# Second feed-forward block in token pieces of 512 and 384, with the output weights stationary and the result transposed

## The chip, the cores and the metric

The kernel runs on one core of a Trainium2 chip. The metric is the device time of one execution in microseconds (us). TensorE (PE) multiplies; its weight loads are shown as an engine of their own (PEld). VectorE (DVE), ScalarE (ACT) and GpSimd (POOL) do the rest, and SyncE (SP) issues the transfers.

## The reference, cut to what matters

```python
attn_out = _attn_ref(q, k, v)              # (2, 12, 448, 64), causal softmax attention
x = attn_out.transpose(0, 2, 1, 3).reshape(896, 768)
h = x @ w_in                               # 768 -> 1024, first block
solu = h * softmax(h)
x = (layernorm(solu) * g_ln) @ w_out       # 1024 -> 768
h = np.maximum(x @ w_in2, 0.0)             # 768 -> 2048, second block
return (h * h @ w_out2).astype(np.float32) # 2048 -> 768, 896 tokens
```

## The kernel before, in words

Precision comes from parts: each float32 operand is held as a high and a low part, and each product is three matmuls that add into the same PSUM place: high by high, high by low, low by high. In every matmul one operand is stationary (the weights that PE loads, 128 columns) and one is moving (it streams through, so many columns).

Attention and the first block run in an order written out by hand (the string `SEQ`). In the first block `h_part` (L474) has the tokens `xT` stationary and `w_in` moving in pieces of 512. `y_part` (L621) has `w_out` stationary, tile `WO[fi]`, and the normalised tokens `lnT` moving, in pieces of 384 (operations y0, tokens 0 to 383) and 512 (y1, tokens 384 to 895). Of the eight `w_out` slices, `load_wo` keeps the first `NWO = 6` in the pool `lnp` and the last two, fi = 6 and 7, in tiles of the pool `wst`, next to those of `w0`. Operation y1.0 runs through fi = 0 to 7, then y1.1, then y1.2: 48 matmuls each, the last 12 of each with fi = 6 and 7.

The second block runs in the order of the code, and this is where the change lies:

- First layer, 16 blocks fi (L744 to L758): `W2[fi]` stationary, the tokens `yT` moving as two halves of `HT` = 448; six chunks c, three part products, two halves: 36 matmuls to a block (L752). `relu_sq` and `relu_lo` turn the result into `G[fi]`, high and low part, tokens along the free axis.
- Second layer, 16 blocks n (L763 to L799), eight for each half of the 768 output columns: `G` stationary, 128 tokens at a time, `W2[n]` moving, 384 columns (L781). A block holds two slices of 128 of the inner 2048 (`TL = 2`), seven token tiles t: 42 matmuls. In the last block of a half the loops are turned, so that one token tile after another is done; L796 copies it out of PSUM (ACT for even t, DVE for odd) and L797 issues its transfer.

The three tiles of `W2` are those of the pool `w0`, `yT` lies in the pool `xy`, and `G` in the pool `gp`. PSUM is four double banks: `bank2` takes the one that has been free longest, `give` returns it. Each block's end calls `next_w2`, which prepares the weights two blocks ahead (DVE, ACT, POOL) and issues the load three ahead on SP.

```python
for e, t in [(e, t) for t in range(NTT) for e in range(TL)] if last else [
    (e, t) for e in range(TL) for t in range(NTT)
]:
```

Of the kernel before, what the change touches and what calls it, by code (L numbers as in the profile page):

```python
# [7 lines left out]
F32 = mybir.dt.float32  # L8
F32R = mybir.dt.float32r
I32 = mybir.dt.int32  # L10
AF = mybir.ActivationFunctionType
ALU = mybir.AluOpType
# [47 lines left out]
def attention_moe_kernel(tc, kq, v, w_in, w_out, g_ln, w_in2, w_out2, out):  # L60
# [6 lines left out]
    nc = tc.nc  # L67
    NP, P, _, S = kq.shape
    D = P // 2
    NT, DM = out.shape  # L70
    H = DM // D
    DFF = w_in.shape[1]
    DFF2 = w_in2.shape[1]
    NC = DM // P
    NF = DFF // P
    NF2 = DFF2 // P
# [3 lines left out]
    NTT = NT // P  # L80
# [3 lines left out]
    def pool(name, bufs=1, side="left", space=None):  # L84
        kw = {"space": space} if space is not None else {}
        return tc.tile_pool(name=name, bufs=bufs, side=side, reuse_waits="tile", **kw)

    def f(ap):
        return ap.bitcast(F32)

    with es:
        const = es.enter_context(pool("const"))
        xy = es.enter_context(pool("xy"))
# [68 lines left out]
        def bank2(nm):  # L162

            pl = slots.pop(0)
            t = pl.tile([P, 2, 512], F32, tag="b", name=nm)
            slot_of[id(t)] = (pl, t)
            return t

        def give(t):
            slots.append(slot_of.pop(id(t))[0])  # L170
# [5 lines left out]
        with att:  # L176
# [463 lines left out]
            yT = []  # L640
# [13 lines left out]
            HD = DM // 2  # L654
            TL = 2
            W2 = {}
# [60 lines left out]
            gp = m2.enter_context(pool("gp", side="right"))  # L717
            tm = m2.enter_context(pool("tm", bufs=2))
            G = [[gp.tile([P, NT], F32R, name=f"g{fi}{s}") for s in range(2)] for fi in range(NF2)]
            HT = NT // 2  # L720
            rl = {}
            hb = {}
            N2 = len(blocks2)
# [1 line left out]
            def next_w2(n):  # L725

                if n + AHEAD < N2:
                    w2_f(n + AHEAD)
                    w2_hi(n + AHEAD)
                    w2_lo(n + AHEAD)  # L730
                if n + 3 < N2 and n + 3 >= NL2:
                    load_w2(n + 3)

            def relu_sq(fi):
                b = hb.pop(fi)
                rl[fi] = tm.tile([P, 2, HT], F32, tag="r", name="relu")
                nc.scalar.activation(rl[fi], b[:, :, 0:HT], AF.Relu)  # L737
                nc.vector.tensor_tensor(rl[fi], b[:, :, 0:HT], rl[fi], ALU.mult)  # L738
                give(b)
                nc.scalar.copy(G[fi][0], rl[fi].rearrange("p a n -> p (a n)"))  # L740

            def relu_lo(fi):
                nc.vector.tensor_tensor(
                    G[fi][1], rl.pop(fi).rearrange("p a n -> p (a n)"), f(G[fi][0]), ALU.subtract  # L744
                )

            for fi in range(NF2):
                b = hb[fi] = bank2("h2")
                for c in range(NC):
                    for w, s in ((0, 0), (0, 1), (1, 0)):  # L750
                        for a in range(2):
                            nc.tensor.matmul(  # L752
                                b[:, a, 0:HT],
                                W2[fi][:, w, c * P : c * P + P],
                                yT[c][s][:, HT * a : HT * a + HT],
                                start=(c == 0 and w == 0 and s == 0),
                                stop=(c == NC - 1 and w == 1),
                            )  # L758
                if fi:
                    relu_sq(fi - 1)  # L760
                next_w2(fi)
                if fi:
                    relu_lo(fi - 1)  # L763
            relu_sq(NF2 - 1)
            relu_lo(NF2 - 1)

            os_ = []
            for n in range(NF2, N2):
                half, fi = blocks2[n]
                if fi == 0:  # L770
                    bs = []
                last = fi == NF2 - TL
                for e, t in [(e, t) for t in range(NTT) for e in range(TL)] if last else [
                    (e, t) for e in range(TL) for t in range(NTT)
                ]:
                    if fi + e == 0 and t % 2 == 0:
                        bs.append(bank2("o"))
                    ob = bs[t // 2][:, t % 2, 0:HD]
                    hi, lo = (W2[n][:, s, HD * e : HD * e + HD] for s in range(2))
                    for s, w, r in ((0, hi, 0), (0, lo, 1), (1, hi, 2)):  # L780
                        nc.tensor.matmul(  # L781
                            ob,
                            G[fi + e][s][:, P * t : P * t + P],
                            w,
                            start=(fi + e == 0 and r == 0),
                            stop=(fi + e == NF2 - 1 and r == 2),
                        )
                    if not (last and e == TL - 1):
                        continue

                    if half == 0:
                        os_.append(xy.tile([P, NT], F32, tag=f"xy{t // 2}{t % 2}", name="o"))
                    if t % 2 or t == NTT - 1:
                        for t_ in range(t - t % 2, t + 1):
                            o = os_[t_][:, HD * half : HD * half + HD]
                            (nc.vector.tensor_copy if t_ % 2 else nc.scalar.copy)(o, bs[t // 2][:, t_ % 2, 0:HD])  # L796
                            nc.sync.dma_start(out[P * t_ : P * t_ + P, HD * half : HD * half + HD], o)  # L797
                        give(bs[t // 2])
                next_w2(n)  # L799


# [36 lines left out]
```

## Time and profile before

| | |
|---|---|
| median of 3 runs | 459.95 us (459.81 to 460.13) |
| profiled execution, span from first to last instruction | 459.8 us |
| PE busy | 452.7 us, 98% of the span |
| granted TensorE clock, mean | 1.000 |
| HBM traffic | 49.16 MB read, 2.80 MB written |

The profiled execution's span is 0.1 us below the median, so that what is worked out on its rows is added to the median. Busy time counts an instruction from its start to its end; the ends of matmuls are modelled, so the distance from one start to the next tells more than the length of one.

### The profile page before, as it was taken

How to read it: one execution, taken by the hardware profiler on the slowest of the kernel's cores; microseconds unless marked ns; L12 is line 12 of the kernel's file. 1: busy time of each engine (PE TensorE's matmuls, PEld its weight loads, DVE VectorE, ACT ScalarE, POOL GpSimd, SP SyncE). 2: the span in 40 equal slices, each digit the busy share in tenths (PEclk: the TensorE clock that was granted, in tenths of full speed). 3: DMA queues.
4: the chain of work that ended last, by engine and by line, in shares of the span. 5: the costliest groups of instructions: out<-in, count | busy, mean ns of one | idle time of the engine just before them, and what ended most of it. 6: DMA issues, size and time to landing. Idle time of an engine off the chain costs nothing.

```text
span 459.8 us, 6525 instructions
## 1 busy us (share of the span) xinstructions
PE 452.7 (98%) x2535; PEld 402.0 (87%) x2535; DVE 275.1 (60%) x524; ACT 164.6 (36%) x213; POOL 120.8 (26%) x122
## 2 busy tenths in 40 slices
PE   8999899999999999999999999999999999999996
PEld 6777676787888899988899999999999999999996
DVE  8889687857569998741346566665763334342321
ACT  3465565533566636231133333424331010310101
POOL 3124547355321011110021322313122231222210
PEclk9999999999999999999999999999999999999999
DMA  8357765232173360000042423324243342734313
GB/s 251 128 154 221 207 159 164 62 79 98 41 280 133 96 248 2 0 1 0 0 138 69 138 80 127 116 91 137 70 137 80 128 113 94 240 90 135 86 52 120
DMA packets 41689, 52.47 MB, mean 114 GB/s; under 512 B 18234, under 2 KB 32314, under 8 KB 41274
## 3 DMA queue, kind: packets, MB, share of 16 engines
q1 hardware_dynamic: 41658, 52.05, 37.1%
q8 instruction: 20, 0.33, 0.3%
q14 instruction: 11, 0.09, 0.1%
HBM read 49.16 MB, written 2.80 MB: 113 GB/s over the span
## 4 chain that ended last, share of the span: by engine, by line
PE 93%; DMA 1%; POOL 1%; ACT 0%; issue 0%; SPq 0%; ACTq 0%; POOLq 0%
PE h L752 25%; PE o L781 25%; PE y L621 13%; PE h L474 13%; PE U L358 9%; PE s L317 4%; PE mxp L257 1%; DMA bc<-d 1%; PE T L599 1%; PE s L325 1%; POOL x L399 1%; PE mxp L284 0%; PE s L333 0%; ACT PP L349 0%; SPq L301 0%
## 5 line engine op out<-in xcount | busy, mean ns | idle before, releaser
L752 PE MATMUL h<-yT,w 128*128 128x448 f32 x576 | 116.9, 365 | 0.0
L781 PE MATMUL o<-w,g 128*128 128x384 f32 x672 | 116.8, 336 | 0.0
L781 PEld LDWEIGHTS o<-w,g 128*128 128x128 f32 x672 | 116.5, 188 | 0.3 <-DVE relu L738 0.2
L752 PEld LDWEIGHTS h<-yT,w 128*128 128x128 f32 x576 | 108.2, 188 | 8.6
L677 POOL TENSOR_TENSOR w<-wf,w 128x768 fp32r<-128x768 f32 x32 | 59.4, 1856 | 206.2 <-ACT w L674 206.2
L149 DVE TENSOR_SCALAR wf<-raw 128x768 int32<-128x768 int32 (+1 forms) x46 | 26.3, 573 | 83.6 <-DMA raw<-in_moe_w_out_dram 58.2
L674 ACT CAST w<-wf 128x768 fp32r<-128x768 f32 x32 | 26.8, 838 | 137.7 <-DVE wf L151 99.4
L474 PE MATMUL h<-w,xT 128*128 128x512 f32 x252 | 59.5, 393 | 0.0
L621 PE MATMUL y<-lnT,w 128*128 128x384 f32 (+1 forms) x288 | 58.9, 365 | 0.0
L621 PEld LDWEIGHTS y<-lnT,w 128*128 128x128 f32 x288 | 51.9, 188 | 5.9
L474 PEld LDWEIGHTS h<-w,xT 128*128 128x128 f32 x252 | 46.8, 188 | 9.6
L358 PE MATMUL U<-PP,VR 128*128 128x448 f32 (+1 forms) x192 | 49.2, 400 | 0.1
L151 DVE SCALAR_TENSOR_TENSOR wf<-raw,wf 128x768 int32<-128x768 int32 (+1 forms) x46 | 47.3, 1029 | 1.6
L150 DVE SCALAR_TENSOR_TENSOR wf<-raw,wf 128x768 int32<-128x768 int32 (+1 forms) x46 | 47.2, 1027 | 1.6
L358 PEld LDWEIGHTS U<-PP,VR 128*128 128x128 f32 x192 | 32.1, 190 | 16.4 <-issue 11.1
L399 POOL TENSOR_TENSOR x<-E,bc 64x448 f32<-64x448 f32 x24 | 31.9, 1328 | 47.2 <-DMA bc<-d 42.7
L272 DVE CUSTOM_DVE_ANT_0 JK<-mxp,MK 112x336 bf16<-112x336 f32 (+2 forms) x96 | 38.8, 446 | 8.5 <-PE mxp L257 7.5
L349 ACT ACTIVATE PP<-s 128x1024 f32<-128x1024 f32 x24 | 24.5, 1023 | 12.9 <-PE s L325 7.2
L738 DVE TENSOR_TENSOR relu<-h,relu 128x896 f32<-128x896 f32 x16 | 17.5, 1092 | 14.6 <-ACT relu L737 14.6
L346 POOL TENSOR_SCALAR_AFFINE_SELECT PP<-PP 128x256 f32<-128x256 f32 (+1 forms) x48 | 19.7, 443 | 21.3 <-ACT PP L349 20.8
L740 ACT CAST g<-relu 128x896 fp32r<-128x896 f32 x16 | 15.1, 942 | 18.6 <-DVE relu L738 18.6
L650 DVE TENSOR_TENSOR yT<-y,yT 128x384 fp32r<-128x384 f32 (+1 forms) x12 | 7.4, 624 | 22.7 <-ACT yT L649 22.7
(75 smaller groups left out, 349.3 us busy)
## 6 DMA issues: line engine op xcount, KB each, us to landing
raw<-in_moe_w_out_dram SPq DMA_DIRECT2D x24, 768.0 KB
raw<-in_moe_w_in_dram SPq DMA_DIRECT2D x16, 768.0 KB
r<-in_kq_dram SPq DMA_DIRECT2D x12, 448.0 KB
VR<-in_v_dram SPq DMA_DIRECT2D x12, 256.0 KB
raw<-in_moe_w_in_dram SPq DMA_DIRECT2D x12, 256.0 KB
raw<-in_moe_w_in_dram SPq DMA_DIRECT2D x3, 1024.0 KB
bc<-d SPq DMA_DIRECT2D x12, 224.0 KB
out_dram<-o SPq DMA_DIRECT2D x14, 192.0 KB
```

The lines of the kernel that those rows point to most:

```text
L149: nc.vector.tensor_scalar(xi, hw, 3, 0x3FFFFFFF, ALU.logical_shift_left, ALU.bitwise_and)
L150: nc.vector.scalar_tensor_tensor(xi, hw, -0x40000000, xi, ALU.bitwise_and, ALU.bitwise_or)
L151: nc.vector.scalar_tensor_tensor(xi, lw, 29, xi, ALU.logical_shift_right, ALU.bitwise_or)
L272: nc.vector.tensor_tensor_reduce(JK[t], b[0:JP, h, o : o + nk], MK[:, S - nk :], 1.0, NEG, ALU.add, ALU.max, mx[i][:, 4 * h + t : 4 * h + ...
L358: nc.tensor.matmul(UB[i][:, h, q0:S], VR[i % 3][:, t, h, :], PP[(2 * i + a) % NPP][:, h, o : o + nq], start=t == 0, stop=t == 2,)
L399: nc.gpsimd.tensor_tensor(x[D * h : D * h + D], e[0:D, h], bc[:, h], ALU.mult)
L474: nc.tensor.matmul(b[:, half, :], xT[c][s][:, t * P : t * P + P], W1[c][:, w, 512 * half : 512 * half + 512], start=(c == 0 and s == 0 and ...
L621: nc.tensor.matmul(b[:, ci, 0:n], WO[fi][:, w, c * P : c * P + P], M["lnT"][a][s][:, fi, :], start=(fi == 0 and w == 0 and s == 0), stop=( ...
L674: nc.scalar.copy(W2[n][:, 0], w_f["2", n])
L677: nc.gpsimd.tensor_tensor(W2[n][:, 1], w_f["2", n], f(W2[n][:, 0]), ALU.subtract)
L752: nc.tensor.matmul(b[:, a, 0:HT], W2[fi][:, w, c * P : c * P + P], yT[c][s][:, HT * a : HT * a + HT], start=(c == 0 and w == 0 and s == 0) ...
L781: nc.tensor.matmul(ob, G[fi + e][s][:, P * t : P * t + P], w, start=(fi + e == 0 and r == 0), stop=(fi + e == NF2 - 1 and r == 2),)
```

## The change

In the first layer the two token pieces become 512 and 384 instead of 448 and 448. In the second layer the roles are exchanged: `W2` is stationary, 128 output columns at a time, and `G` moves in the same two pieces. A half then has three output tiles d of 128 columns by 896 tokens, with 36 matmuls to a block (L751, one helper `products` for both layers). The output is written transposed, 768 by 896, in two transfers to a tile, and the host transposes it back.

```diff
-                rl[fi] = tm.tile([P, 2, HT], F32, tag="r", name="relu")
-                nc.scalar.activation(rl[fi], b[:, :, 0:HT], AF.Relu)
-                nc.vector.tensor_tensor(rl[fi], b[:, :, 0:HT], rl[fi], ALU.mult)
+                rl[fi] = tm.tile([P, NT], F32, tag="r", name="relu")
+                bf = b.rearrange("p a n -> p (a n)")[:, 0:NT]
+                nc.scalar.activation(rl[fi], bf, AF.Relu)
+                nc.vector.tensor_tensor(rl[fi], bf, rl[fi], ALU.mult)
...
+            CHUNKS = ((0, 512), (512, NT - 512))
+
+            def products(b, w, c, ops, first, last):
+
+                for r, (wp, s) in enumerate(((0, 0), (0, 1), (1, 0))):
+                    for a, (o, n) in enumerate(CHUNKS):
+                        nc.tensor.matmul(
+                            b[:, a, 0:n],
+                            w[:, wp, c : c + P],
+                            ops[s][:, o : o + n],
+                            start=first and r == 0,
+                            stop=last and r == 2,
+                        )
...
                 for c in range(NC):
-                    for w, s in ((0, 0), (0, 1), (1, 0)):
-                        for a in range(2):
-                            nc.tensor.matmul(
-                                b[:, a, 0:HT],
-                                W2[fi][:, w, c * P : c * P + P],
-                                yT[c][s][:, HT * a : HT * a + HT],
...
+                    products(b, W2[fi], c * P, yT[c], c == 0, c == NC - 1)
...
-            os_ = []
+            ND = NC // 2
             for n in range(NF2, N2):
                 half, fi = blocks2[n]
                 if fi == 0:
-                    bs = []
+                    bs = [bank2("o") for d in range(ND)]
                 last = fi == NF2 - TL
...
-                    if fi + e == 0 and t % 2 == 0:
-                        bs.append(bank2("o"))
-                    ob = bs[t // 2][:, t % 2, 0:HD]
-                    hi, lo = (W2[n][:, s, HD * e : HD * e + HD] for s in range(2))
-                    for s, w, r in ((0, hi, 0), (0, lo, 1), (1, hi, 2)):
-                        nc.tensor.matmul(
-                            ob,
-                            G[fi + e][s][:, P * t : P * t + P],
-                            w,
...
+                order = [(e, d) for e in range(TL) for d in range(ND)]
+                for e, d in sorted(order, key=lambda x: x[1]) if last else order:
+                    products(bs[d], W2[n], HD * e + P * d, G[fi + e], fi + e == 0, fi + e == NF2 - 1)
                     if not (last and e == TL - 1):
                         continue
...
-                    if t % 2 or t == NTT - 1:
-                        for t_ in range(t - t % 2, t + 1):
-                            o = os_[t_][:, HD * half : HD * half + HD]
-                            (nc.vector.tensor_copy if t_ % 2 else nc.scalar.copy)(o, bs[t // 2][:, t_ % 2, 0:HD])
-                            nc.sync.dma_start(out[P * t_ : P * t_ + P, HD * half : HD * half + HD], o)
-                        give(bs[t // 2])
+                    c = ND * half + d
+                    o_ = xy.tile([P, NT], F32, tag=f"xy{c}0", name="o")
+                    for a, (o, m) in enumerate(CHUNKS):
+                        (nc.vector.tensor_copy if a else nc.scalar.copy)(o_[:, o : o + m], bs[d][:, a, 0:m])
+                        nc.sync.dma_start(out[P * c : P * c + P, o : o + m], o_[:, o : o + m])
+                    give(bs[d])
```

What this does to the order shows at three places. In a row the output stands ahead of the arrow; behind it the first operand is the moving one, the second the weights.

On PE, at the first block of the first layer, before:

```order
L752 MATMUL h2_2299<-yT00_2113,w_2133 128x448 x2
L752 MATMUL h2_2299<-yT01_2114,w_2133 128x448 x2
L752 MATMUL h2_2299<-yT00_2113,w_2133 128x448 x2
L752 MATMUL h2_2299<-yT10_2115,w_2133 128x448 x2
L752 MATMUL h2_2299<-yT11_2116,w_2133 128x448 x2
```

and in the changed kernel:

```order
L751 MATMUL h2_2299<-yT00_2113,w_2133 128x512
L751 MATMUL h2_2299<-yT00_2113,w_2133 128x384
L751 MATMUL h2_2299<-yT01_2114,w_2133 128x512
L751 MATMUL h2_2299<-yT01_2114,w_2133 128x384
L751 MATMUL h2_2299<-yT00_2113,w_2133 128x512
L751 MATMUL h2_2299<-yT00_2113,w_2133 128x384
```

The number of matmuls, their weights and their operands stay; equal lengths become lengths that alternate.

On PE, at the first block of the second layer (o is a PSUM tile, w a tile of W2, g00 and g01 the high and low part of G[0]), before:

```order
L781 MATMUL o_3115<-w_3053,g00_2267 128x384 x2
L781 MATMUL o_3115<-w_3053,g01_2268 128x384
L781 MATMUL o_3115<-w_3053,g00_2267 128x384 x2
L781 MATMUL o_3115<-w_3053,g01_2268 128x384
L781 MATMUL o_3122<-w_3053,g00_2267 128x384 x2
```

and in the changed kernel:

```order
L751 MATMUL o_3115<-g00_2267,w_3053 128x512
L751 MATMUL o_3115<-g00_2267,w_3053 128x384
L751 MATMUL o_3115<-g01_2268,w_3053 128x512
L751 MATMUL o_3115<-g01_2268,w_3053 128x384
L751 MATMUL o_3115<-g00_2267,w_3053 128x512
L751 MATMUL o_3115<-g00_2267,w_3053 128x384
L751 MATMUL o_3116<-g00_2267,w_3053 128x512
```

The two operands have changed places, and a half fills three double banks instead of four.

On SP, at the end of the program (raw is a block of W2 on its way in, o the output):

```order
 L124 DMA raw<-in_moe_w_out_dram 128x2x768 x6
-L797 DMA out_dram<-o 128x384 x7
-L834 UNCONDITIONAL_BRANCH
+L786 DMA out_dram<-o 128x512
+L786 DMA out_dram<-o 128x384
+L786 DMA out_dram<-o 128x512
+L786 DMA out_dram<-o 128x384
+L786 DMA out_dram<-o 128x512
+L786 DMA out_dram<-o 128x384
+L823 UNCONDITIONAL_BRANCH
```

Seven output transfers become six; the last two belong to one tile, whose 512-piece is copied by ACT and whose 384-piece by DVE.

## Rows read from the trace of the kernel before

**Rows 1.** The page: busy time of PE, and the granted clock in 40 slices.

```profile
PE 452.7 (98%) x2535; PEld 402.0 (87%) x2535; DVE 275.1 (60%) x524; ACT 164.6 (36%) x213; POOL 120.8 (26%) x122
...
PEclk9999999999999999999999999999999999999999
```

**Rows 2.** The chain that ended last, from 290 us on: start, us, what.

```profile
289.83 49.66 PE h L752 x245
339.49 116.70 PE o L781 x672
456.19 0.02 issue
456.21 0.48 ACT o L796
```

**Rows 3.** The page's groups: xcount | busy us, mean ns | idle before it.

```profile
L752 PE MATMUL h<-yT,w 128*128 128x448 f32 x576 | 116.9, 365 | 0.0
L781 PE MATMUL o<-w,g 128*128 128x384 f32 x672 | 116.8, 336 | 0.0
```

**Rows 4.** Timeline of PE, 139 to 143.3: start, us, instructions merged.

```profile
138.83 4.25 PE L474 MATMUL h<-w,xT 128*128 128x512 f32 x18
```

**Rows 5.** Timeline of PE, 163 to 178, y0 with fi from 0 on.

```profile
162.67 15.07 PE L621 MATMUL y<-lnT,w 128*128 128x384 f32 x86
```

**Rows 6.** Timeline of PE, 187.1 to 189.6, y0 with fi = 7.

```profile
186.85 2.98 PE L621 MATMUL y<-lnT,w 128*128 128x384 f32 x16
```

**Rows 7.** Timeline of PE, 212 to 219, y1.2 with fi from 0 on.

```profile
211.62 7.64 PE L621 MATMUL y<-lnT,w 128*128 128x512 f32 x33
```

**Rows 8.** Timeline of PE, 219.9 to 222.2, y1.2 with fi = 6 and 7.

```profile
219.55 2.96 PE L621 MATMUL y<-lnT,w 128*128 128x512 f32 x12
```

**Rows 9.** Instructions by form, 139 to 143.3, 187.1 to 189.6 and 219.9 to 222.2.

```profile
L474 PE MATMUL h<-w,xT 128*128 128x512 f32 x18 | 4.2, 389 | 0.0
...
L621 PE MATMUL y<-lnT,w 128*128 128x384 f32 x16 | 3.0, 338 | 0.0
...
L621 PE MATMUL y<-lnT,w 128*128 128x512 f32 x12 | 3.0, 395 | 0.0
```

**Rows 10.** Line L474 from 160.5 to 161.9: durations ns min/median/max; last row is the longest.

```profile
L474 PE MATMUL h<-w,xT x8: 389/389/397, 160.1 to 161.7; 128*128 128x512 f32 x8
```

**Rows 11.** Instructions by form, 189.7 to 191.0, the change from y0 to y1.

```profile
L621 PE MATMUL y<-lnT,w 128*128 128x512 f32 x6 | 1.6, 393 | 0.0
L621 PE MATMUL y<-lnT,w 128*128 128x384 f32 x1 | 0.3, 332 | 0.0
```

**Rows 12.** Line L781, 338 to 345: durations ns min/median/max; idle time ended by.

```profile
L781 PE MATMUL o<-w,g x32: 333/336/442, 339.3 to 344.9; 128*128 128x384 f32 x32
its engine sat idle before it (us, times) until:
  DVE relu L738: 0.2, 1
```

**Rows 13.** Timeline of the end, 449 to 460; idle before and what ended it in brackets.

```profile
455.17 0.48 ACT L796 COPY o<-o 128x384 f32<-128x384 f32 x1 [1.60 <-PE o L781]
455.68 0.56 DVE L796 COPY o<-o 128x384 f32<-128x384 f32 x1 [1.52 <-ACT o L796]
456.21 0.48 ACT L796 COPY o<-o 128x384 f32<-128x384 f32 x1 [0.56 <-PE o L781]
```

**Rows 14.** ACT by form, 150 to 225: the casts of yT.

```profile
L649 ACT CAST yT<-y 128x512 fp32r<-128x512 f32 x6 | 3.5, 588 | 24.3 <-PE y L621 22.0 <-DVE yT L650 2.3
L649 ACT CAST yT<-y 128x384 fp32r<-128x384 f32 x6 | 2.8, 482 | 5.1 <-DVE yT L650 5.0
```

**Rows 15.** Transfers from 451 to 460 in 40 slices, GB/s.

```profile
GB/s 0 0 0 0 0 0 314 362 246 376 369 82 0 0 0 246 375 280 328 389 130 0 0 0 150 382 314 287 369 383 376 335 27 0 0 0 0 0 0 0
```

More of the change, by code (lines that the diff above doesn't have):

```diff
@@ L69, in attention_moe_kernel @@
     D = P // 2
-    NT, DM = out.shape
+    DM, NT = out.shape
     H = DM // D
@@ L719, in attention_moe_kernel @@
             G = [[gp.tile([P, NT], F32R, name=f"g{fi}{s}") for s in range(2)] for fi in range(NF2)]
-            HT = NT // 2
             rl = {}
@@ L735, in relu_sq @@
                 b = hb.pop(fi)
-                rl[fi] = tm.tile([P, 2, HT], F32, tag="r", name="relu")
-                nc.scalar.activation(rl[fi], b[:, :, 0:HT], AF.Relu)
-                nc.vector.tensor_tensor(rl[fi], b[:, :, 0:HT], rl[fi], ALU.mult)
+                rl[fi] = tm.tile([P, NT], F32, tag="r", name="relu")
+                bf = b.rearrange("p a n -> p (a n)")[:, 0:NT]
+                nc.scalar.activation(rl[fi], bf, AF.Relu)
+                nc.vector.tensor_tensor(rl[fi], bf, rl[fi], ALU.mult)
                 give(b)
-                nc.scalar.copy(G[fi][0], rl[fi].rearrange("p a n -> p (a n)"))
+                nc.scalar.copy(G[fi][0], rl[fi])
             def relu_lo(fi):
-                nc.vector.tensor_tensor(
-                    G[fi][1], rl.pop(fi).rearrange("p a n -> p (a n)"), f(G[fi][0]), ALU.subtract
-                )
+                nc.vector.tensor_tensor(G[fi][1], rl.pop(fi), f(G[fi][0]), ALU.subtract)
+            CHUNKS = ((0, 512), (512, NT - 512))
[9 more added lines that the diff above has]
+                        )
             for fi in range(NF2):
@@ L749, in attention_moe_kernel @@
                 for c in range(NC):
-                    for w, s in ((0, 0), (0, 1), (1, 0)):
-                        for a in range(2):
-                            nc.tensor.matmul(
-                                b[:, a, 0:HT],
-                                W2[fi][:, w, c * P : c * P + P],
-                                yT[c][s][:, HT * a : HT * a + HT],
-                                start=(c == 0 and w == 0 and s == 0),
-                                stop=(c == NC - 1 and w == 1),
-                            )
+                    products(b, W2[fi], c * P, yT[c], c == 0, c == NC - 1)
                 if fi:
@@ L770, in attention_moe_kernel @@
                 if fi == 0:
-                    bs = []
+                    bs = [bank2("o") for d in range(ND)]
                 last = fi == NF2 - TL
-                for e, t in [(e, t) for t in range(NTT) for e in range(TL)] if last else [
-                    (e, t) for e in range(TL) for t in range(NTT)
-                ]:
-                    if fi + e == 0 and t % 2 == 0:
-                        bs.append(bank2("o"))
-                    ob = bs[t // 2][:, t % 2, 0:HD]
-                    hi, lo = (W2[n][:, s, HD * e : HD * e + HD] for s in range(2))
-                    for s, w, r in ((0, hi, 0), (0, lo, 1), (1, hi, 2)):
-                        nc.tensor.matmul(
-                            ob,
-                            G[fi + e][s][:, P * t : P * t + P],
-                            w,
-                            start=(fi + e == 0 and r == 0),
-                            stop=(fi + e == NF2 - 1 and r == 2),
-                        )
+                order = [(e, d) for e in range(TL) for d in range(ND)]
+                for e, d in sorted(order, key=lambda x: x[1]) if last else order:
+                    products(bs[d], W2[n], HD * e + P * d, G[fi + e], fi + e == 0, fi + e == NF2 - 1)
                     if not (last and e == TL - 1):
                         continue
-                    if half == 0:
-                        os_.append(xy.tile([P, NT], F32, tag=f"xy{t // 2}{t % 2}", name="o"))
-                    if t % 2 or t == NTT - 1:
-                        for t_ in range(t - t % 2, t + 1):
-                            o = os_[t_][:, HD * half : HD * half + HD]
-                            (nc.vector.tensor_copy if t_ % 2 else nc.scalar.copy)(o, bs[t // 2][:, t_ % 2, 0:HD])
-                            nc.sync.dma_start(out[P * t_ : P * t_ + P, HD * half : HD * half + HD], o)
-                        give(bs[t // 2])
+                    c = ND * half + d
[4 more added lines that the diff above has]
+                    give(bs[d])
                 next_w2(n)
@@ L832 @@
     B, H, S, D = inputs["q"].shape
-    out = nc.dram_tensor("out_0_dram", (B * S, H * D), F32, kind="ExternalOutput").ap()
+    out = nc.dram_tensor("out_0_dram", (H * D, B * S), F32, kind="ExternalOutput").ap()
     with tile.TileContext(nc) as tc:
@@ L836 @@
     r = run_bass_kernel_spmd(nc, [arrays], core_ids=[0])
-    return r.results[0]["out_0_dram"]
+    return np.ascontiguousarray(r.results[0]["out_0_dram"].T)
```

## The prediction, on record before the changed kernel ran

> **What bounds the kernel now.** I read the page first. PE is busy 98% of the span, every other engine 60% or less, and the granted clock is at its upper level, 2.4 GHz, in all 40 slices [rows 1]. Then the chain of waits: from 290 us on it is PE alone, 49.66 us of the first layer's L752, then 116.70 us of L781, then a copy on ACT and the last transfer [rows 2]. Nothing ahead of PE is waited for here, so the change can act in two ways only: by the time from one matmul's start to the next, and by what follows the last matmul.
>
> Busy shares do not give that time, since a matmul's end is modelled: L752's matmuls last 365 ns each but take 116.9 us together, 203 ns each [rows 3]. I therefore work with the **spacing** from start to start. For a stretch of equal matmuls it is (length of the stretch less the mean length of one) / (number less one). Before, the spacing is 49.66 / 245 = 202.7 ns for 448 columns, so a pair of halves takes 405.4 ns, and 116.70 / 672 = 173.7 ns for 384 columns [rows 2].
>
> **What the new lengths cost.** The changed kernel has matmuls of 512 and 384 columns. Earlier stages of this trace have both, although never in alternation.
>
> - 512 columns, L474, weights xT and moving w_in: (4.25 - 0.389) / 17 = 227 ns [rows 4, 9].
> - 384 columns, y0 with w_out slices from the pool lnp as weights: (15.07 - 0.336) / 85 = 173.3 ns [rows 3, 5]; 336 ns is the mean length of such a one in L781 too. 512 columns, y1 with such slices: (7.64 - 0.389) / 32 = 226.6 ns [rows 7, 9].
> - The same two stages with fi = 6 and 7, whose slices lie in the tiles of wst: 512 columns (2.96 - 0.395) / 11 = 233.2 ns [rows 8, 9], 384 columns (2.98 - 0.338) / 15 = 176.1 ns [rows 6, 9].
>
> So there is a cheap spacing and a dear one. The cheap pair 512 + 384 takes 226.8 + 173.3 = 400.1 ns, the dear pair 233.2 + 176.1 = 409.3 ns. Subtracting cheap 384 from cheap 512 gives 53.4 ns for 128 columns, 0.417 ns each, which is one column a cycle at 2.4 GHz. A cheap matmul thus costs its columns and some 13 ns; 448 columns would be 200 ns on that line, and the first layer takes 2.7 ns more.
>
> What makes the dear ones dear the trace does not say. It shows where they occur: weights read from the w tiles, while the moving operand is lnT, outside the pools xy and w0. L474 has both operands in xy and w0 and is cheap. L781 has the w tiles as moving operand and G as weights, and at 173.7 ns it is cheap too.
>
> **First layer.** 576 matmuls stay 576, now 288 pairs. Weights W2 (w0) and moving yT (xy) lie in the same two pools as L474's operands, with the roles exchanged, so I take the cheap pair: 288 x (405.4 - 400.1) = **1.5 us gained**. The bounds: the dear pair would lose 288 x 3.9 = 1.1 us. Alternation may have its own price: the last 512 ahead of the first 384 lasted 397 ns instead of 389 [rows 10], so its spacing is about 235, and at the change from y0 to y1 the last 384 lasted 332 instead of 336, spacing about 170, and the 512s behind it 393, about 231 [rows 11]. By 235 + 170 = 405 ns nothing is gained; by 231 + 173, a third of the gain remains. At these places weights and lengths change together, so they bound the price and do not fix it.
>
> **Second layer.** 672 matmuls of 384 columns become 576, or 288 pairs: the columns are the same, 258,048. The weights are now W2 in w tiles and the moving operand is G, which lies in neither xy nor w0: the dear combination is the nearest row. 288 x 409.3 ns = 117.9 us against 116.70: **1.2 us lost**. With the cheap pair it would be 115.2 us, 1.5 us gained. One stall goes with either: now the fourth double bank of the layer waits 0.2 us for the last relu_sq [rows 12]; three banks need no such wait, because they had been given back a block earlier. That stall is inside the 116.70 and absent in the new sum.
>
> **The end.** Now the last token tile has one copy, 0.48 us on ACT, and then its transfer [rows 13]. In the changed kernel the last output tile has 896 columns: ACT copies 512, DVE then 384. The chain of copies stays serial, as now, where DVE begins 0.03 us behind ACT's end on the same double bank [rows 13]. ACT's 512 columns I price by its cast of yT, 588 ns against 482 for 384 [rows 14]; DVE's by its copy, 0.56 us [rows 13]. So the last transfer is issued 0.11 + 0.03 + 0.56 = 0.70 us later behind the last matmul. It also queues behind a piece a third larger: 192 KB takes some 0.6 us at the 280 to 390 GB/s of the last slices [rows 15], and was issued 0.45 us behind its predecessor, so it waits 0.15 us; 256 KB takes 0.8 us and is issued 0.59 us ahead, which makes 0.2. Together **0.75 us lost**; bounds 0.5 (if the transfer ahead ends early) and 1.0.
>
> **What costs nothing.** relu_sq has the same 896 elements, only over two full banks; it lies beside PE, which does not wait for it inside the layer [rows 3]. A block's length stays about 7.3 us (42 x 173.7 ns or 18 pairs), so the preparation of weights two blocks ahead on DVE, ACT and POOL keeps its lead, and so do the loads on SP behind the six output transfers of the first half. If that cover were gone, it would show as PE waiting for POOL or a load at the blocks' starts; a block's whole preparation fits beside one block now with DVE busy 60%. At the change of half, the next three banks hold one that was free all along and two given back one output tile earlier, 2.4 us or more ahead.
>
> **The sum.** -1.5 + 1.2 + 0.75 = +0.45 us on a span of 459.8; added to the median, 460.4 us. 0.2% of this kernel, 0.92 us, is about what a measurement can tell from no change, so this is the same.
>
> **The rivals.**
>
> *The place of the weights has no price in the second layer.* Both layers then run cheap pairs: -1.5 - 1.5 + 0.75 = -2.2 us, **457.7 us**, faster. For it: L781 runs cheap although its operands lie in different pools, and in the stretches read here only w_out slices 6 and 7 are dear. Against it: both lengths turn dear at these slices, with the same operand moving and the same clock as their cheap neighbours.
> The Trainium skill, page "TensorE: Matmul & The Clock Gate", section "Step-by-step: what each phase is for", says that PE has two independent read ports, so that loading the next weights takes no read bandwidth from the running matmul. By that rule no placing of weights could cost anything, and this rival would be the forecast; the trace does not agree with it between [rows 7] and [rows 8], where only the weights' tiles change and the spacing goes from 226.6 to 233.2 ns.
>
> *The first layer gains nothing or loses as well* (slower). Its weights are W2 in w tiles, too, and its 202.7 ns lies halfway between the cheap line's 200.0 and 204.7 on the line through the dear rows. If alternation costs 405 ns a pair there, the sum is -0.1 + 1.2 + 0.75 = +1.85, **461.8 us**; if the dear pair holds in both layers, 1.1 + 1.2 + 0.75 = +3.1, **463.0 us**. It decides (over 0.92 us lost, with the second layer dear) from a first-layer pair of about 402 ns on.
>
> *The lengths do nothing.* A pair takes 405 ns in both layers, whatever the weights: 0 in the first, 288 x 405.2 = 116.7 in the second, and the end alone remains: +0.7, 460.6 us, the same.
>
> **How the numbers follow.** Forecast 0.42, no price for the weights 0.18, first layer without gain or dear 0.29, lengths without effect 0.11. The predicted time is the forecast's. The range reaches from the first rival, 457.7, to the middle of the second, 462.4, and leaves out its dear half and little more, under 2 in 10. The forecast's own range is 459.6 to 461.2, from the bounds of the end and some 2 ns to a pair. Faster by over 0.2%: 0.19 (the first rival, and the forecast's edge); slower by over 0.2%: 0.33 (the second, and the other edge); within: 0.48.
>
> **What would show it right or wrong.** Stretches of PE in the changed trace: first layer 115.2 us from its first start to the second layer's, second layer 117.9 us to the last matmul. Lengths of 389 and 336 ns in the first layer and about 395 and 338 in the second would confirm cheap and dear; 389 and 336 in both mean the first rival, 397 with 332 in turn mean a price of alternation. DVE's last copy should start 0.03 us behind ACT's, and the span end some 4.4 us behind the last matmul's modelled end instead of 3.6. The prediction is wrong if PE waits at block starts, if the clock falls, or if the two lengths behave together as neither does alone: no row here has them in alternation, and that is its weakest step.

## The result, and the profile after

The changed kernel takes 463.29 us (median of 6 runs) against 460.25 in runs beside it: ratio 1.0064, interval 1.0053 to 1.0076, 2.4 to 3.5 us slower. The forecast was 460.4 us and no measurable change. Each run's time here lies some 1.75 us above its span (462.85 over 461.1), so the profile of before with its span of 459.8 was a longer execution than the median; it reached the second block at 222.75 us and the changed kernel at 221.23. I therefore compare stretches, not spans.

The page of the changed kernel, busy time and granted clock:

```profile
PE 454.2 (99%) x2439; PEld 386.1 (84%) x2439; DVE 274.3 (59%) x524; ACT 164.4 (36%) x211; POOL 120.1 (26%) x122
...
PEclk9999999999999999999999999999999999999999
```

PE is the bound as before [rows 1] and the clock has not moved. The chain that ended last, from 215 us on (start, us, what):

```profile
221.23 119.02 PE h L751 x576
340.25 116.37 PE o L751 x576
456.62 0.02 issue
456.64 0.59 ACT o L785
457.24 0.02 issue
457.26 0.56 DVE o L785
```

The same chain of before, from 215 us on, has for the first layer

```profile
222.75 116.74 PE h L752 x576
```

Against this and [rows 2], the first layer takes 2.28 us more, the second 0.33 less. The end, from the last matmul's modelled end to the span's end, takes 461.07 - 456.62 = 4.45 us instead of 459.81 - 456.19 = 3.62, 0.83 more. The sum, +2.78 us, is within the interval.

The groups by form of the changed kernel (xcount | busy, mean ns):

```profile
L751 PE MATMUL h<-yT,w 128*128 128x512 f32 x288 | 114.6, 398 | 0.0
L751 PE MATMUL o<-g,w 128*128 128x512 f32 x288 | 112.7, 391 | 0.0
L751 PE MATMUL h<-yT,w 128*128 128x384 f32 x288 | 97.3, 338 | 0.0
L751 PE MATMUL o<-g,w 128*128 128x384 f32 x288 | 97.0, 337 | 0.0
```

The idle column is 0.0: PE waited for nobody. The whole difference within the layers is in the spacing. A pair takes 119.02 / 288 = 413.3 ns in the first layer and 404.1 in the second. Neither is the cheap pair (400.1) or the dear one (409.3) that was read from the stages ahead, and the mean lengths, 398 and 338 ns in the first layer, 391 and 337 in the second, are none of the pairs of lengths that the prediction named as signs.

### The profile page after: what moved, and what is told of

Same layout as the page of the kernel before. It is cut to its first block, busy times and chain, and to the rows that moved or that the text cites. A ratio compares the mean times of both kernels' runs of the same rounds, so it can differ in the third digit from the quotient of the medians.

```text
span 461.1 us, 6327 instructions
## 1 busy us (share of the span) xinstructions
PE 454.2 (99%) x2439; PEld 386.1 (84%) x2439; DVE 274.3 (59%) x524; ACT 164.4 (36%) x211; POOL 120.1 (26%) x122
## 4 chain that ended last, share of the span: by engine, by line
PE 93%; DMA 2%; ACT 1%; POOL 0%; issue 0%; SPq 0%; DVE 0%; ACTq 0%; POOLq 0%
PE h L751 26%; PE o L751 25%; PE y L621 13%; PE h L474 13%; PE U L358 9%; PE s L317 3%; PE mxp L257 1%; PE T L599 1%; DMA bc<-d 1%; DMA raw<-in_moe_w_in_dram 1%; PE s L325 1%; POOL x L399 0%; PE s L333 0%; PE mxp L284 0%; ACT PP L349 0%
## 5 line engine op out<-in xcount | busy, mean ns | idle before, releaser
L751 PE MATMUL h<-yT,w 128*128 128x512 f32 x576 | 119.2, 368 | 0.0
L751 PEld LDWEIGHTS h<-yT,w 128*128 128x128 f32 x576 | 104.8, 188 | 14.3
L751 PE MATMUL o<-g,w 128*128 128x512 f32 x576 | 116.5, 364 | 0.0
L751 PEld LDWEIGHTS o<-g,w 128*128 128x128 f32 x576 | 104.4, 188 | 11.9
L474 PE MATMUL h<-w,xT 128*128 128x512 f32 x252 | 59.5, 393 | 0.0
L474 PEld LDWEIGHTS h<-w,xT 128*128 128x128 f32 x252 | 46.8, 188 | 9.6
```

The source lines that it names most:

```text
L474: nc.tensor.matmul(b[:, half, :], xT[c][s][:, t * P : t * P + P], W1[c][:, w, 512 * half : 512 * half + 512], start=(c == 0 and s == 0 and ...
L751: nc.tensor.matmul(b[:, a, 0:n], w[:, wp, c : c + P], ops[s][:, o : o + n], start=first and r == 0, stop=last and r == 2,)
```

## The experiments

In the table "first" and "second" are the two layers in us, from the chain of each profile; "end" runs from the last matmul's modelled end to the span's end. In the built program the tiles of W2, yT and xT start at multiples of 64 bytes, those of G, lnT and the w_out slices 0 to 5 at 32 bytes past one. "Apart" is by how many bytes the weights and the moving operand of a layer differ in this.

| kernel | order of lengths | first (apart) | second (apart) | end |
|---|---|---|---|---|
| before | 448; 384 | 116.74 (0) | 116.70 (32) | 3.62 |
| changed | alternating | 119.02 (0) | 116.37 (32) | 4.45 |
| e1 | alternating; 384 | 119.02 (0) | 116.52 (32) | 3.63 |
| e2 | 448; alternating | 116.74 (0) | 116.37 (32) | 4.43 |
| e3 | runs of 3 | 117.44 (0) | 117.78 (32) | 4.45 |
| e4 | alternating | 117.12 (32) | 119.04 (0) | 4.45 |
| e5 | runs of 18 | 116.25 (0) | 118.09 (32) | 4.45 |
| e6 | runs of 18 | 117.13 (32) | 116.31 (0) | 4.46 |
| e7 | runs of 18 | 116.22 (0) | 116.35 (0) | 4.47 |
| e8 | runs of 18 | 116.22 (0) | 116.35 (0) | 3.66 |
| e10 | runs of 36 | 115.73 (0) | 115.90 (0) | 3.67 |
| e11 | 448; 384 | 116.73 (0) | 116.59 (0) | 3.64 |

The same instructions at the same places came out alike in different programs: 116.74, 116.74 and 116.73 us for the 448s of before, e2 and e11, and 116.22 and 116.35 in both e7 and e8. The second layer of before and e1 differs by 0.18, the stall of [rows 12], which e1 does not show. Differences of some tenths of a us between layers can thus be read from one profile each.

**e1 and e2: one layer each.** In e1 the kernel of before has this changed (cut), and `relu_sq` and `relu_lo` read the two pieces as one row, as in the changed kernel:

```diff
-                        for a in range(2):
+                        for a, (o, n) in enumerate(((0, 512), (512, NT - 512))):
                             nc.tensor.matmul(
-                                b[:, a, 0:HT],
+                                b[:, a, 0:n],
                                 W2[fi][:, w, c * P : c * P + P],
-                                yT[c][s][:, HT * a : HT * a + HT],
+                                yT[c][s][:, o : o + n],
```

> Only the first layer has the new pieces (512 and 384); the second layer and the output are those of before. In the profile of the changed kernel the first layer took 119.0 us (pairs of 237.4 + 175.9 = 413.3 ns) against 116.7 before. If alternating lengths with these weights are the cause, this kernel's first layer takes 119.0 us again, its second layer 116.7, and the time is 2.3 us over before. Rival: the first layer's spacing is a product of the new second layer or of the layout of the program; then the first layer stays at 115 to 117 us and the time within 0.7 us of before.

e2 is the changed kernel with the first layer's 448s, and `relu_sq` and `relu_lo` of before (cut):

```diff
-                    products(b, W2[fi], c * P, yT[c], c == 0, c == NC - 1)
+                    products(b, W2[fi], c * P, yT[c], c == 0, c == NC - 1, ((0, 448), (448, 448)))
```

> Only the second layer and the output are the new ones; the first layer has its 448s. In the changed kernel the second layer took 116.37 us against 116.70, and the end behind the last matmul's start 4.80 us against 3.97. If each layer's spacing is its own, the first layer takes 116.7, the second 116.4, the end 4.8, and the time is 0.5 us over before. Rival: the transposed output costs more than the span shows, since the changed kernel's timed runs lie 1.75 us above their spans; then the time is 2 us over before at a span only 0.5 us longer.

e1: 462.62 us against 460.51, ratio 1.0048 (1.0035 to 1.0062); first layer 119.02 us. e2: 460.97, ratio 1.0012 (1.0003 to 1.0020); second layer 116.37, end 4.43. Each layer's time is its own, and the two changes, 0.48% and 0.12%, nearly add up to the changed kernel's 0.64%. e2's +0.46 us is the end's 0.8 less the layer's 0.3; the rival of a hidden cost of the transposed output falls. The first layer's pieces carry most of the loss, the end the rest.

**e3: runs of three.**

```diff
-                for r, (wp, s) in enumerate(((0, 0), (0, 1), (1, 0))):
-                    for a, (o, n) in enumerate(CHUNKS):
+                for a, (o, n) in enumerate(CHUNKS):
+                    for r, (wp, s) in enumerate(((0, 0), (0, 1), (1, 0))):
```

> The changed kernel with the two loops of products exchanged: three matmuls of 512, then three of 384, instead of alternating. If the alternation itself has the price (each change of length some 6 to 13 ns), the first layer falls from 119.0 to between 116 and 117.5 us, and the second to between 115 and 116. Rival: the price hangs on the operands' places and not on the order; then the first layer stays at 119.0 and the second at 116.4.

463.23 us in one run. The first layer fell to 117.44, as the price of alternation had it, but the second rose by 1.4 us to 117.78. Neither theory had that: the order matters, and in opposite directions in the two layers.

**e4: 32 unused bytes.** One unused tile, ahead of the pools of the W2 tiles, moves these by 32 bytes:

```diff
         xT = xy_tiles("xT")
+        es.enter_context(pool("pad")).tile([P, 8], F32, name="pad")
```

> The changed kernel with an unused tile of 32 bytes between the pool xy and the pools behind it, so that the w tiles begin 32 bytes later and G, yT and the w_out slices 0 to 5 stay. If the start addresses of weights and moving operand against each other (modulo 64 bytes) set the spacing, the dear stretches of the first block (w_out slices 6 and 7: 233 and 176 ns) become cheap (227 and 173), and both layers of the second block change by 1 us or more. Rival: it is the order of lengths or the pool as such; then those stretches stay at 233 and 176, and the layers at 119.0 and 116.4 us.

465.31 us in one run. The layers exchanged their roles: the second, whose operands were now equal modulo 64 bytes, took 119.04 us, what the first had taken in the changed kernel, and the first 117.12, 0.75 more than the second had taken there. In the first block the 512s of L475 (L474 before), now 32 bytes apart, went from 227 to 233 ns; their whole group, by form, before the pad (changed kernel) and with it:

```profile
L474 PE MATMUL h<-w,xT 128*128 128x512 f32 x252 | 59.5, 393 | 0.0
```

```profile
L475 PE MATMUL h<-w,xT 128*128 128x512 f32 x252 | 60.9, 398 | 0.0
```

That is 1.4 us for 32 bytes, in code that the change does not touch. The last w_out slices became cheap at 512 columns (e7 below shows the same). At 384 they did not as expected, since the pad had moved the operand lnT of y0 as well: y0, now 32 bytes apart throughout, takes 177 ns in slices that were at 173. So the start addresses modulo 64 bytes, with the order of lengths, set the spacing of the 512s; for the 384s they are not the whole rule, since L781 runs at 173.7 ns with its operands 32 bytes apart.

**e5, e6, e7: runs of 18, with the places varied.** Each block runs its 512s first, then its 384s; in the last block of a half six and six for each output tile (cut):

```diff
                 for c in range(NC):
-                    products(b, W2[fi], c * P, yT[c], c == 0, c == NC - 1)
+                for a in range(2):
+                    for c in range(NC):
+                        products(b, W2[fi], c * P, yT[c], c == 0, c == NC - 1, a)
...
+                order = [(a, e, d) for a in range(2) for e in range(TL) for d in range(ND)]
```

> The changed kernel with each block's 18 matmuls of 512 first and its 18 of 384 behind them, in both layers (6 and 6 for each tile in the last block of a half). Nothing else moves; W2 and yT start at the same place modulo 64 bytes, G 32 bytes off. Theory: with equal lengths in a row, operands that start equally modulo 64 bytes run at the cheap spacing (227 and 173) and those 32 bytes off at the dear one (233 and 176), and it is the alternation that turned this round in the changed kernel. Then the first layer takes 115.2 to 115.9 us and the second 117.6 to 118.1. Rival 1: both lengths in one kernel cost, in whatever order; the first layer stays above 117. Rival 2: the second layer's spacing does not depend on the place; it falls to 115.5 with the first.

e6 adds e4's pad to it.

> The same with the 32 unused bytes ahead of the w tiles: now W2 and yT are 32 bytes apart modulo 64, W2 and G equal. By the theory of places the two layers exchange their times: first 117.6 to 118.1, second 115.2 to 115.9. By the rival that the pool or the stage sets the spacing, they stay as without the pad.

e7 has these two instead of the pad, which bring G, lnT and the w_out slices to multiples of 64 bytes:

```diff
+            es.enter_context(pool("padr", side="right")).tile([P, 8], F32, name="padr")
...
+                M["tmp"].tile([P, 8], F32, tag="pad", name="pad", bufs=1)
```

> The same without that pad, but 32 unused bytes at the start of the right-hand pools and of the pool tmp, so that all weights and moving operands of both feed-forward blocks start equally modulo 64 bytes. By the theory both layers are cheap, 115.2 to 115.9 us each, and the last w_out slices (fi = 6 and 7) in the first block take 227 and 173 ns as their neighbours do. By the rival the second layer stays at 117.6 or more.

One run each: 462.33, 462.73 and 460.43 us. The chains of e5, e6 and e7:

```profile
221.77 116.25 PE h L750 x576
338.02 118.09 PE o L750 x576
```

```profile
223.04 117.13 PE h L751 x576
340.17 116.31 PE o L751 x576
```

```profile
221.62 116.22 PE h L752 x576
337.85 116.35 PE o L752 x576
```

In runs the direction is that of the first block's rows: a layer is cheap with equal places, dear with places 32 bytes apart. The pad exchanges the layers (e5 to e6): it is the place of one operand against the other that counts, since with G at 32 bytes the second layer takes 118.09 us with W2 at 0 and 116.31 with W2 at 32 as well. Aligning G alone takes 1.74 us off the second layer (e5 to e7), with the same instructions in the same order. Aligned, the runs came out 0.3 to 0.5 us above the upper end expected, e6's first layer 0.5 below its lower end, since its 384s were cheap at 32 bytes apart (mean length 336 ns, not 338). In e7 the w_out slices 6 and 7 are at the cheap spacing at 512 columns; here the timeline of PE, 218.6 to 221.1, and the same stretch by form:

```profile
218.29 3.11 PE L623 MATMUL y<-lnT,w 128*128 128x512 f32 x13
```

```profile
L623 PE MATMUL y<-lnT,w 128*128 128x512 f32 x13 | 3.1, 389 | 0.0
```

(3.11 - 0.389) / 12 = 226.8 ns against 233.2 before [rows 8].

At 384 columns e7 missed what was expected of the first block. In y0, whose places are now equal in all slices, the spacing of the first slices went from 173.3 ns [rows 5] to (7.36 - 0.338) / 40 = 175.6 (41 matmuls from 162.81 us on). The group by form, before and in e7:

```profile
L621 PE MATMUL y<-lnT,w 128*128 128x384 f32 x144 | 26.0, 338 | 0.0
```

```profile
L623 PE MATMUL y<-lnT,w 128*128 128x384 f32 x144 | 26.2, 340 | 0.0
```

Equal places are thus not cheap for every run of equal lengths.

**e8: the end.** The last output tile's 384-piece gets the fourth double bank, so that its 512-piece can be copied and sent while PE still works (cut):

```diff
-                    products(bs[d], W2[n], HD * e + P * d, G[fi + e], fi + e == 0, fi + e == NF2 - 1, a)
+                    if fi + e == 0 and own and a:
+                        b2 = bank2("o")
+                    b = b2 if own and a else bs[d]
+                    products(b, W2[n], HD * e + P * d, G[fi + e], fi + e == 0, fi + e == NF2 - 1, a)
...
+                        (nc.scalar.copy if own or not x else nc.vector.tensor_copy)(o_[:, o : o + m], b[:, x, 0:m])
```

> The same, and the last output tile has its 384-piece in the fourth double bank, so that ACT copies and sends the 512-piece while PE still works on the 384-piece, and nothing waits for another engine's copy at the end. If the serial copies make up the end's loss, the time from the last matmul's start to the span's end falls from 4.80 us to between 3.8 and 4.0. With both layers cheap that makes 0.9 + 0.7 us less in the layers and nothing lost at the end: 1.5 us under the kernel before, ratio about 0.9967. If the end does not depend on the copies it stays at 4.8, and the gain is 0.7 us.

459.60 us against 460.29, ratio 0.9983 (0.9974 to 0.9992). The end, in the changed kernel's timeline from 455 us on:

```profile
456.64 0.59 ACT L785 COPY o<-o 128x512 f32<-128x512 f32 x1 [1.84 <-PE o L751]
457.26 0.56 DVE L785 COPY o<-o 128x384 f32<-128x384 f32 x1 [1.87 <-ACT o L785]
```

and in e8's from 452 us on:

```profile
453.02 0.59 ACT L793 COPY o<-o 128x512 f32<-128x512 f32 x1 [0.80 <-PE o L752]
454.06 0.48 ACT L793 COPY o<-o 128x384 f32<-128x384 f32 x1 [0.46 <-PE o L752]
```

In the built program of the changed kernel DVE's copy waits for a semaphore of ACT's copy, although the pieces lie in two banks. Two copies in series behind PE became one, and the end went from 4.47 to 3.66 us, against 3.62 before: the serial copies were nearly its whole loss. The layers gained 0.9 us against before rather than the 1.6 expected, since a run of 18 is not wholly at the cheap spacing.

**e10: runs of 36.** Every second block takes its 384s first, and so does the middle output tile of a half's last block (cut):

```diff
-                for a in range(2):
+                for a in (1, 0) if fi % 2 else (0, 1):
```

> The aligned kernel with the early copy, and every second block (and the middle output tile of a last block) takes its 384s first, so that a length changes half as often. In the aligned runs of 18 a 512 took 229 ns on average against 226.7 in a long stretch, and a 384 174.8 against 173.4: some 0.07 us to a block, 1 us to a layer of 16. Theory: that is the price of a change of length, paid over the matmuls behind it. Then each layer falls from 116.2 to 115.6 to 115.9 us, and the time is 1.3 to 1.9 us below before (ratio 0.996 to 0.997). Rival: those matmuls are slower for another reason in each block (the new weights, the semaphores at its end); then the layers stay at 116.2 and the ratio at 0.9983.

458.63 us against 460.35, ratio 0.9959 (0.9945 to 0.9973), 1.2 to 2.5 us faster than before. Both layers fell by 0.45 to 0.49 us for half as many changes of length, as expected. The starts in e5's trace show where a change is paid with aligned operands: in a block of its first layer the last 512 ahead of a 384 takes 227 ns, as in a long run, but the first nine 512s behind the change take 224 to 236, and the rest 226 to 227.

```profile
221.56 115.73 PE h L752 x576
337.29 115.90 PE o L752 x576
```

**e11: the places alone.** The kernel of before with e7's two pads.

> The kernel before with nothing but the 32 unused bytes at the two places that align the operands. Its first layer had W2 and yT aligned already and its second ran at the cheap 173.4 ns with G 32 bytes off. If what was gained came from runs of 512 and 384 and not from the places as such, the first layer stays at 116.7 and the second at 116.3 to 116.6 us. Rival: the places alone gain; one of the layers falls by 0.5 us or more.

460.56 us in one run against 460.35; layers 116.73 and 116.59 us. Aligning gains nothing for the 448s, which were aligned, nor for the 384s of L781, which at 173.7 ns were cheap 32 bytes apart. What e8 and e10 gained comes from runs of 512 and 384 with aligned operands.

## Why the prediction was wrong

**The bound and the method held.** PE alone, no waits at block starts, the clock at its upper level: all as read from [rows 1, 2].

**The step that failed** is the price of the first layer: "so I take the cheap pair: 288 x (405.4 - 400.1) = 1.5 us gained". It took spacings measured in runs of equal length and added a 512 and a 384. In alternation with aligned operands the pair costs 413.3 ns, 2.28 us lost in the layer, more even than the dear pair given as the bound. The place was read rightly (L474's operands are aligned, as these are), but alternation turns its sign: aligned operands, cheapest in runs (400 ns a pair; 403.6 in runs of 18), are dearest in alternation (413.3 in the changed kernel and e1, and in e4's other layer). The prediction called this its weakest step and bounded alternation by single changes of length [rows 10, 11], at 405 ns; in these rows the operands' places changed at the same moment, and a single change is no alternation. In e5, where the places stay, the last 512 ahead of a 384 takes 227 ns instead of that row's 235; the price lies in the matmuls behind a change.

**The second layer** was mis-sized by the same step. 1.2 us lost was forecast from the dear pair; measured are 0.33 us gained at 404.1 ns, of which 0.2 is the stall for relu_sq that went, as said [rows 12]; e1, which still has four double banks, does not show it either, so that three banks as the reason are not shown. The dear spacing itself was rightly seen: in runs of 18 (e5) the layer takes 118.09 us against the 117.9 worked out.

**The end** was right: 0.75 us lost forecast, 0.83 measured, with DVE 0.03 us behind ACT, and e8 shows the serial copies as the cause.

**The rivals.** The slower one ("if the dear pair holds in both layers", 463.0 us) is near the time by chance: it has +1.1, +1.2 and +0.75 for the layers and the end, measured are +2.3, -0.3 and +0.8. The first rival, that the place has no price, falls by e5 against e7: 1.74 us for 32 bytes. The third, that the lengths do nothing, falls by e1: 2.28 us in the first layer. The Trainium skill, page "TensorE: Matmul & The Clock Gate", section "Step-by-step: what each phase is for", gives PE two independent read ports, so that loading the next weights takes no read bandwidth from the running matmul. By that the place of the weights against the moving operand should have no price; these runs do not agree: it changes a pair by 3 to 6 ns in runs of 18 (e5, e6 and e7) and by 7 to 9, the other way, in alternation (changed kernel and e4).

**What stays open.** Why alignment and alternation act on each other was not settled; nothing in these profiles shows what PE waits for within a matmul. The 384s follow more than the address modulo 64 bytes: L781 and e6's first layer are cheap at 32 bytes apart, y0 in e4 is not, and y0 in e7 is dearer aligned than it was. What ran before may play a part, which no run tested: in e7's trace the distances of starts in y0 repeat 177, 174 and 175 ns up to a group of transposes and 175, 182, 176, 173 and 174 behind it, with lengths, order and places modulo 64 bytes the same.

## What to carry to other kernels

Take a matmul's price from the spacing of starts, and from a stretch that has the same order of lengths and the same start addresses of weights and moving operand; a sum of spacings from uniform runs does not price a mixed order. Where PE is busy all the time, keep equal lengths in long runs and try the places of both operands against each other: here equal places modulo 64 bytes in the second block's layers, with the last copy taken off the end, turned a change that lost 0.6% into one that gains 0.4%, while y0's 384s got dearer by them. Two copies of one PSUM tile behind the last matmul ran in series; a tile of its own for the last piece lets the first copy run under PE.

## What the runs showed of the hardware that was not expected

An unused tile of 32 bytes moved 1.4 us in a stage that the change does not touch (59.5 to 60.9 us for 252 matmuls of 512 columns, e4), and another took 1.74 us off the second layer (e5 to e7). With operands equal modulo 64 bytes a pair of 512 and 384 columns cost 413.3 ns in alternation and 402 in runs of 36, with the same instructions in another order; 32 bytes apart it cost 404.1 to 406.7 ns in alternation and 406.7 to 410.0 in runs of 18 (e6's first layer, e5's second); what fits one order of lengths is thus the wrong place for the other. With aligned operands a change of length is paid over the matmuls behind it, some 0.03 us each by e8 and e10 (0.49 us for 15 changes fewer in the first layer).
